# Issuing the stores and the v loads from SyncE, and moving the v loads and the second v cast of one batch, in a fused attention and feed-forward kernel

## The chip, the cores and the metric

The kernel runs on one core of one Trainium2 chip. The metric is the device time of one execution in microseconds (us). Each kernel was run several times, in rounds in which it alternates with the kernel before on the same chip. The span that a profile shows is about 1.8 us shorter than the device time of the same run.

Engines have short names in the profile: PE is TensorE (matmuls), PEld its weight loads, DVE is VectorE, ACT is ScalarE, POOL is GpSimd, SP is SyncE. A trailing q (ACTq, SPq) means the instruction queue of that engine, here the issuing of a DMA. L427 is line 427 of the kernel file. From its first edit on, the changed file is one line shorter, so L427 of before is L426 of after, and so on; from the last edit on, near the end of the file, it is three lines longer. The experiments have line numbers of their own.

## The reference, cut to what matters

```python
# per batch b (8) and head (8): cosine-weighted linear attention over 576 positions, head size 64
q_p = [relu(q) * cos, relu(q) * sin];  k_p = the same of k
kv  = k_p^T @ v;  z = sum over positions of k_p
attn = (q_p @ kv) / (q_p @ z + 1e-6)
# then on all 4608 tokens (512 channels, 1536 hidden)
xn  = attn / rms(attn) * g
out = (silu(xn @ w_gate) * (xn @ w_val)) @ w_out
```

Inputs and output are float32; the kernel multiplies in bfloat16.

## The kernel before: the parts that matter

The work is cut into blocks. Block b is the feed-forward network of the 512 main tokens of batch b; block 8 is that of the last 64 tokens of every batch. A block has 16 slots: slots 0 to 11 compute one slice of the hidden layer each (four matmuls into psG, four into psV, a silu on ScalarE giving sg, a product on VectorE giving hT), and slots 12 to 15 compute one quarter of the output each (12 matmuls into psC, a copy to osb on ScalarE, a store). The attention of batch b+1 is woven into the slots of block b, and the loads for batch b+2 too.

```python
def load_piece(which, b, p):
    if which != "q":
        eng = nc.scalar if (which, b) == ("v", 3) else nc.sync
        load_kv(which, b, p, p + 1, eng=eng)
    ...

def v_cast(eng, b, r0=0, r1=4, j0=0, j1=NJ):      # raw v (float32) -> vvm (bfloat16)
    ...
def kvz_mm(b, banks, rs=(0, 4)):                  # kv and z: psA <- vvm, kpm (72 matmuls)
    ...
def nd_pe(b, j, pst):                             # numerator, denominator: psA <- kvzs, qpT (8 matmuls)
    ...
def nd_post(b, j, pst):                           # VectorE: rec, reciprocal, xt = numerator * rec
    ...
def x_norm(b, j):                                 # VectorE: xn
    ...
def x_tr_dma(b, j):                               # transpose by DMA, from SyncE: xnT <- xn
    nc.sync.dma_start_transpose(out=x_dst(b, j), in_=xn_of[(b, j)][:, :])

def out_store(eng, blk, j, bank):
    osb = four.tile([P, DM], FP32, name="osb", tag="osb")
    copy(eng, osb[:, :], bank)
    if blk < 8:
        rows = out[blk * S : blk * S + 512, :].rearrange("(p j) m -> p j m", j=4)
        (nc.scalar if blk else nc.sync).dma_start(out=rows[:, j, :], in_=osb[:, :])
    ...

for nb in range(2, B):                            # attention of batch nb, in block b
    b = nb - 1
    ...
    if nb == 3:
        vb, vn = b, 1
    ...
    at(vb, vn, "post", v_cast, V, nb, *LOW)
    at(vb, vn + 1 + (nb == 3), "post", v_cast, V, nb, *HIGH)
    ...
for nb in range(3, B):                            # loads of batch nb, in block b
    b = nb - 2
    for i, which in enumerate(("k", "v", "q")):
        for p in range(5 if which == "q" else 4):
            n = (p, 7 + p, 6 + p)[i] if b == 1 else 5 * i + p
            at(b + n // 16, n % 16, "post", load_piece, which, nb, p)
```

Batch 3 is the exception in this schedule. Its v is loaded in four pieces by ScalarE in slots 7 to 10 of block 1, and its second cast (HIGH) follows the first by two slots, where in the other batches it follows by one.

## Time and profile before

| | before |
|---|---|
| device time | 330.03 us median of 3 runs, 330.01 to 330.08 |
| span of the profile | 328.8 us (the profiled run took 330.61 us, 0.6 us more than the median) |
| TensorE, VectorE, ScalarE busy | 97%, 56%, 54% |
| TensorE idle between 60 and 314 us | 1.63 us and 1.23 us |

The page gives the busy times of the engines (microseconds, share of the span, number of instructions) and the shares of the chain of work that ended last.

```profile
PE 319.3 (97%) x2445; PEld 162.3 (49%) x2445; DVE 185.7 (56%) x412; ACT 177.8 (54%) x366; POOL 32.2 (10%) x67
PE 86%; DVE 5%; DMA 3%; ACT 3%; issue 1%; ACTq 1%; SPq 0%; DVEq 0%
```

TensorE is nearly always busy, so only the moments in which it waits can pay. Busy time by stretches finds them. The columns are the stretch, its length, and the busy time of each engine; the last three are the granted clock, the DMA share and GB/s.

```profile
80.00:84.00 4.00, 2.37 (x19) 1.12 (x18) 2.92 (x6) 1.39 (x4) 0.55 (x1) 1.00 1.05 257
93.00:117.00 24.00, 22.77 (x199) 11.38 (x198) 16.55 (x34) 12.94 (x26) 2.15 (x4) 1.00 0.80 177
```

The view of waits names the releasers (total us, times, longest us):

```profile
ACT sg L436 <- DMA rq<-in_q_dram: 1.9, 1, 1.9
PE psA L311 <- DVE xt L365: 1.6, 1, 1.6
PE psA L283 <- DVE vvm L266: 1.2, 1, 1.2
```

The timeline shows how they hang together. Columns: start, duration, engine, line, operation, count, and in brackets the idle time before it and its releaser. First gap A, in block 1, slot 12:

```profile
79.10 0.33 ACTq L79 DMA_DIRECT2D rv<-in_v_dram  x1
79.47 1.46 PE L447 MATMUL psC<-wo,hT 128*128 128x512 bf16 x6
79.48 0.60 ACT L436 ACTIVATE sg<-psG 128x512 f32<-128x512 f32 x1 [1.91 <-DMA rq<-in_q_dram]
80.11 0.69 DVE L442 TENSOR_TENSOR hT<-psV,sg 128x512 bf16<-128x512 f32 x1 [2.78 <-ACT sg L436]
80.72 0.74 DVE L388 SCALAR_TENSOR_TENSOR xn<-xt,rs,gb 128x512 bf16<-128x512 f32 x1
81.81 0.69 DVE L365 TENSOR_TENSOR xt<-psA,rec 128x512 f32<-128x512 f32 x1
82.56 0.40 PE L311 MATMUL psA<-kvzs,qpT 128*128 128x65 bf16 x8 [1.63 <-DVE xt L365]
92.34 1.03 PE L427 MATMUL psG<-xnT,wg 128*128 128x512 bf16 x4
```

ScalarE runs its instructions in order. The third load of v could not be issued before 79.10, the silu behind it therefore started late, and from there the delay ran over hT, xn and xt to TensorE. Gap B is in block 2, slot 4:

```profile
98.38 1.03 PE L427 MATMUL psV<-xnT,wv 128*128 128x512 bf16 x4
99.34 0.75 PE L283 MATMUL psA<-vvm,kpm 64*128 64x65 bf16 x36
100.52 0.75 DVE L266 CAST vvm<-rv 128x1152 bf16<-128x1152 f32 x1
101.33 0.75 PE L283 MATMUL psA<-vvm,kpm 64*128 64x65 bf16 x36 [1.23 <-DVE vvm L266]
102.01 1.04 PE L427 MATMUL psG<-xnT,wg 128*128 128x512 bf16 x4
```

The second half of kv of batch 3 needs the HIGH cast, which comes in slot 3 of this block, one slot too late.

### The profile page before, as it was taken

The page shows a single profiled execution, that of the slowest core. Times are in us where ns is not written, and L with a number is a line of the kernel's source. Part 1 is how long each engine was busy: PE and PEld are TensorE (multiplying, and loading weights), DVE is VectorE, ACT ScalarE, POOL GpSimd, SP SyncE. Part 2 cuts the span into 40 slices and gives each one's busy share as a digit, 9 for nine tenths or more (in the row PEclk, how much of TensorE's full clock was granted, in tenths as well). Part 3 has the DMA queues.
Part 4 walks back from the last instruction along what each step waited for, and adds up shares of the span by engine and source line. Part 5 has one row for each costly group of instructions (what it writes and reads, how often), then busy time and mean ns, then how long its engine had stood idle before and what let it go on. Part 6 is the DMA issues. An engine that isn't in the chain of part 4 may idle for free.

```text
span 328.8 us, 6430 instructions
## 1 busy us (share of the span) xinstructions
PE 319.3 (97%) x2445; PEld 162.3 (49%) x2445; DVE 185.7 (56%) x412; ACT 177.8 (54%) x366; POOL 32.2 (10%) x67
## 2 busy tenths in 40 slices
PE   8999999998998999999999999999999999999995
PEld 3587465553444444544454445444554444444443
DVE  5875758776755775577257745773577234203410
ACT  6863875963675447545764576447654233223321
POOL 1660112000100100011001100110011000000000
PEclk9999999999999999999999999999999999999999
DMA  7999999899959676966698588967621400020014
GB/s 262 233 197 266 315 179 335 292 201 262 189 135 208 184 168 189 221 192 165 194 212 197 149 204 198 195 168 206 135 56 32 130 32 0 19 110 1 0 35 96
DMA packets 80338, 53.91 MB, mean 164 GB/s; under 512 B 51377, under 2 KB 67761, under 8 KB 80306
## 3 DMA queue, kind: packets, MB, share of 16 engines
q1 hardware_dynamic: 68176, 39.34, 49.7%
q0 software_dynamic: 6880, 4.72, 10.0%
q10 hardware_dynamic: 5250, 9.44, 9.4%
q8 instruction: 19, 0.31, 0.4%
q14 instruction: 13, 0.11, 0.1%
HBM read 37.75 MB, written 9.44 MB: 144 GB/s over the span
## 4 chain that ended last, share of the span: by engine, by line
PE 86%; DVE 5%; DMA 3%; ACT 3%; issue 1%; ACTq 1%; SPq 0%; DVEq 0%
PE psC L447 26%; PE psG L427 25%; PE psV L427 24%; PE psA L283 3%; PE psA L311 2%; DMA rk<-in_k_dram 2%; PE psG L447 1%; DMA rq<-in_q_dram 1%; PE psG L567 1%; PE psV L567 1%; PE psO L567 1%; DVE vvm L266 1%; DVE qp L212 1%; DVE kpm L212 1%; ACT sg L436 1%
## 5 line engine op out<-in xcount | busy, mean ns | idle before, releaser
L442 DVE TENSOR_TENSOR hT<-psV,sg 128x512 bf16<-128x512 f32 x102 | 70.3, 690 | 95.1 <-PE psV L427 82.0
L436 ACT ACTIVATE sg<-psG 128x512 f32<-128x512 f32 x102 | 60.7, 595 | 65.9 <-PE psG L427 63.9
L427 PE MATMUL psG<-xnT,wg 128*128 128x512 bf16 (+1 forms) x368 | 92.9, 375 | 0.1
L427 PE MATMUL psV<-xnT,wv 128*128 128x512 bf16 (+1 forms) x368 | 92.7, 374 | 0.0
L447 PE MATMUL psC<-wo,hT 128*128 128x512 bf16 x396 | 89.4, 379 | 0.0
L427 PEld LDWEIGHTS <-wv 128*128 128x128 bf16 x416 | 40.7, 98 | 47.4
L447 PEld LDWEIGHTS <-hT 128*128 128x128 bf16 x420 | 40.3, 98 | 46.7
L427 PEld LDWEIGHTS <-wg 128*128 128x128 bf16 x416 | 38.5, 98 | 41.0 <-DVE xnT L266 0.4
L381 POOL TENSOR_TENSOR rs<-ms,mhalf 128x1 f32<-128x1 f32 x36 | 19.8, 551 | 203.0 <-ACT scr L376 203.0
L388 DVE SCALAR_TENSOR_TENSOR xn<-xt,rs,gb 128x512 bf16<-128x512 f32 x36 | 26.8, 746 | 19.1 <-POOL rs L381 19.1
L376 ACT ACTIVATE scr<-xt 128x513 bf16<-128x513 f32 x36 | 22.8, 634 | 25.3 <-DVE xt L365 23.7
L264 ACT COPY osb<-psC 128x512 f32<-128x512 f32 (+1 forms) x33 | 19.0, 577 | 31.9 <-PE psC L447 30.7
L210 ACT ACTIVATE kpm<-rk,tab 128x256 bf16<-128x256 f32 (+1 forms) x78 | 31.9, 476 | 7.0 <-ACT osb L264 5.4
L365 DVE TENSOR_TENSOR xt<-psA,rec 128x512 f32<-128x512 f32 x35 | 24.2, 692 | 1.2
L212 DVE TENSOR_SCALAR kpm<-rk,tab 128x256 bf16<-128x256 f32 (+1 forms) x84 | 22.3, 330 | 2.4 <-DMA rk<-in_k_dram 2.4
L210 ACT ACTIVATE qp<-rq,tab 128x512 bf16<-128x512 f32 x32 | 22.4, 713 | 0.0
L311 PEld LDWEIGHTS <-qpT 128*128 128x128 bf16 x248 | 11.6, 98 | 8.5 <-issue 2.2
L212 DVE TENSOR_SCALAR qp<-rq,tab 128x512 bf16<-128x512 f32 x32 | 15.2, 487 | 0.0
L311 PE MATMUL psA<-kvzs,qpT 128*128 128x65 bf16 x248 | 12.8, 194 | 1.9 <-DVE xt L365 1.6
L427 PE MATMUL psG<-xnt_tail,wg 128*128 128x512 bf16 x48 | 12.3, 379 | 0.0
L427 PE MATMUL psV<-xnt_tail,wv 128*128 128x512 bf16 x48 | 12.3, 379 | 0.0
L283 PEld LDWEIGHTS <-kpm 64*128 64x128 bf16 x576 | 9.9, 95 | 4.7 <-issue 4.1
(89 smaller groups left out, 170.8 us busy)
## 6 DMA issues: line engine op xcount, KB each, us to landing
out_dram<-osb ACTq DMA_DIRECT2D x28, 256.0 KB, 3.1
rk<-in_k_dram SPq DMA_DIRECT2D x20, 288.0 KB, 3.7
rq<-in_q_dram SPq DMA_DIRECT2D x20, 256.0 KB, 4.3
rv<-in_v_dram SPq DMA_DIRECT2D x17, 288.0 KB, 3.1
rk<-in_k_dram SPq DMA_DIRECT2D x2, 1152.0 KB, 8.9
rq<-in_q_dram SPq DMA_DIRECT2D x2, 1024.0 KB, 9.4
rv<-in_v_dram SPq DMA_DIRECT2D x3, 576.0 KB, 9.5
wo<-in_moe_w_out_dram POOLq DMA_DIRECT2D x4, 384.0 KB, 7.9
```

Of the source, the lines that this page charges most:

```text
L210: nc.scalar.activation(out=out_ap, in_=in_ap, func=AF.Relu, scale=scale)
L212: eng.tensor_scalar(out=out_ap, in0=in_ap, scalar1=scale, scalar2=0.0, op0=ALU.mult, op1=ALU.max)
L283: nc.tensor.matmul(banks[c][:, r * E : (r + 1) * E], lhsT=kp_main[b][lo : lo + 64, j, r, :], rhs=vvm[b % 2][lo : lo + 64, r, j, :], start= ...
L311: nc.tensor.matmul(o[:, g, i, :], lhsT=qpT[(b, 0)][:, h, j * P : (j + 1) * P], rhs=kvz_of(b, h), start=True, stop=True,)
L365: nc.vector.tensor_tensor(out=xt[:, 0:DM].rearrange("p (b h d) -> p b h d", b=2, d=D), in0=o[:, :, :, 0:D], in1=rec[:, :, :].unsqueeze(3). ...
L376: nc.scalar.activation(out=scr[:, :], in_=xt[:, 0 : DM + 1], func=AF.Square, scale=1.0 / math.sqrt(DM), accum_out=ms[:, :],)
L381: nc.gpsimd.tensor_tensor(out=rs[:, :], in0=ms[:, :], in1=mhalf[:, :], op=ALU.pow)
L388: nc.vector.scalar_tensor_tensor(out=xn[:, :], in0=x_of[(b, j)][:, 0:DM], scalar=rs_of[(b, j)][:, :], in1=gb[:, :], op0=ALU.mult, op1=ALU. ...
L427: nc.tensor.matmul(pst[bank][:, cols[0] : cols[1]], lhsT=w[:, t, n * P : (n + 1) * P], rhs=x[:, t, cols[0] : cols[1]], start=(t == 0), sto ...
L436: nc.scalar.activation(out=sg[:, :], in_=psG[bank][:, :], func=AF.Silu)
L442: nc.vector.tensor_tensor(out=hTs[blk][:, n, :], in0=psV[bank][:, :], in1=sg[:, :], op=ALU.mult)
L447: nc.tensor.matmul(bank, lhsT=hTs[blk][:, n, j * P : (j + 1) * P], rhs=wo[:, n, :], start=(n == 0), stop=(n == NNT - 1),)
```

## The change

Its intent is to free ScalarE of all DMA issuing in blocks 1 to 8 (but for two stores at the very end, which stay), to load v of batch 3 only after the transposes of batch 2 have been issued, and to have both v casts of batch 3 done before TensorE needs them.

```diff
     def load_piece(which, b, p):
         if which != "q":
-            eng = nc.scalar if (which, b) == ("v", 3) else nc.sync
-            load_kv(which, b, p, p + 1, eng=eng)
+            load_kv(which, b, p, p + 1)
 ...
-            (nc.scalar if blk else nc.sync).dma_start(out=rows[:, j, :], in_=osb[:, :])
+            nc.sync.dma_start(out=rows[:, j, :], in_=osb[:, :])
 ...   # block 8: two stores of 64 rows each
-                nc.scalar.dma_start(
+                nc.sync.dma_start(
 ...
-        at(vb, vn + 1 + (nb == 3), "post", v_cast, V, nb, *HIGH)
+        at(vb, vn + 1, "post", v_cast, V, nb, *HIGH)
 ...
         for i, which in enumerate(("k", "v", "q")):
+            if (which, nb) == ("v", 3):
+                at(b, 13, "post", load_kv, "v", nb, *LOW)
+                at(b, 14, "post", load_kv, "v", nb, *HIGH)
+                continue
             for p in range(5 if which == "q" else 4):
-                n = (p, 7 + p, 6 + p)[i] if b == 1 else 5 * i + p
+                n = (0, None, 6)[i] + p if b == 1 else 5 * i + p
```

More of the change, by code (lines that the diff above doesn't have):

```diff
@@ L69, with load_kv @@
     raw = {}
-    def load_kv(which, b, r0=0, r1=4, j0=0, j1=NJ, eng=nc.sync):
+    def load_kv(which, b, r0=0, r1=4, j0=0, j1=NJ):
         key = (which, b)
@@ L78, in load_kv @@
         src = {"k": k, "v": v}[which]
-        return eng.dma_start(
+        return nc.sync.dma_start(
             out=raw[key][:, r0:r1, j0 * D : j1 * D],
```

## The prediction

> What bounds it now. The page gives TensorE 319.3 us busy of a 328.8 us span (97%) at full granted clock; the chain that ended last is 86% TensorE. Only a gap on TensorE can pay. The table of busy time by stretches shows two between 60 and 314 us: 1.63 us in 80-84 (2.37 of 4.00 busy) and 1.23 us in 93-117 (22.77 of 24.00).
>
> Gap A (80.9 to 82.6 us, block 1 slot 12). The timeline has ScalarE issue the third load of v of batch 3 at 79.10; it stood 1.91 us before its next silu, which the view of waits puts on a DMA of rq. That silu (79.48) delayed hT (80.11), xn (80.72) and xt (ends 82.50), and the eight psA matmuls of tile 3 waited for xt. From the start of psC (79.47) to the next block's first psG (92.34) 12.87 us pass; the chain's clean lengths (10.36 for 48 psC matmuls, 0.24 and 0.37 for the small groups) give 10.97. Gap A costs 1.9 us.
>
> Gap B (100.1 to 101.3, block 2 slot 4). The second half of kvz of batch 3 waited 1.23 us for the HIGH v cast, which VectorE ran in slot 3 (100.52). psV to psG over kvz takes 3.63 us here, 2.23 in block 3: gap B costs 1.4 us.
>
> What changes. (1) No v load in ScalarE's stream in slots 7-10: the silu can start near 77.6. By the traced steps (silu start to hT start 0.63, on to xt end 2.39) xt ends at 80.6; TensorE needs it at 80.8. Gap A closes with 0.1 us to spare. (2) HIGH cast in slot 2: ends near 99.6 in old time; its matmuls are due at 100.0. Gap B closes. (3) 34 stores leave ScalarE, 0.34 to 0.5 us each, some 13 us; ScalarE is 54% busy and no TensorE gap waits on a store: worth nothing. (4) SyncE gains them. In a block of 33.6 us it then issues about 21 us (transposes 1.2 us, loads 0.57 us, stores 0.34 us each). It has room, but issues in order: q pieces of slots 12-13 stand behind stores that wait for osb. In block 2 the last large q piece would issue near 124 instead of 122 us, land near 128.5, and be wanted near 129.3. (5) v of batch 3 in two 576 KB loads would issue near 88 and 89 us and land near 92.5 and 95 (estimate from 4.4 us for such a load of rk and 200 to 250 GB/s); casts come near 95 and 97.
>
> The Trainium skill, "DMA: Bandwidth & Descriptors", section "Issuing engines are not separate DMA queues", says that all issuers share 16 DMA engines and another issuer saves only issue time. The trace shows that issue time, 0.34 us a store; I expect no bandwidth effect.
>
> On the critical path: 1.9 + 1.4 = 3.3 us. Predicted 326.8 us, 326.4 to 328.2 eight times in ten. Chances: faster by over 2% 0.01, within 2% 0.97, slower 0.02.
>
> Right, if: no silu waits for a DMA of rq, psA waits for neither xt nor vvm after 60 us, TensorE stays near 319 us busy in a span near 325.5. Wrong, if: v of batch 3 lands after its cast is due (vvm waits for a DMA near 95 us, hT behind it); q pieces held behind stores make qp wait for rq at the start of blocks 3 to 6; or xt still ends too late.

## The result, and the profile after

| | before | after |
|---|---|---|
| device time, median of 5 runs | 330.01 us (329.73 to 330.08) | 326.83 us (326.63 to 327.37) |
| ratio after/before | | 0.9908 (95%: 0.9893 to 0.9922) |
| span of the profile | 328.8 us | 325.0 us |

A ratio is the mean time of one kernel's fast runs over the mean of the other's fast runs of the same rounds, so it is not quite the ratio of the medians. The gain of 3.18 us (330.01 - 326.83) is 1.0%, and is well clear of the noise.

The same views after. First the page:

```profile
PE 316.5 (97%) x2410; PEld 161.8 (50%) x2445; DVE 185.8 (57%) x412; ACT 176.7 (54%) x366; POOL 31.9 (10%) x67
PE 91%; DMA 2%; ACT 2%; DVE 2%; issue 1%; SPq 1%
```

Only 2410 of the 2445 matmuls have a record here, so the busy time of TensorE is too low. A later profile of the same kernel (e12_change_again) has all 2445 and gives 318.7 us in a span of 325.5 us. The work is the same as before (319.3 us); what went is the waiting. Busy time by stretches says the same, since what is missing here in 93-117 are absent records (216 matmuls; the later profile has 220 in this stretch, and 24.00 us busy):

```profile
80.00:84.00 4.00, 4.00 (x27) 1.98 (x26) 3.03 (x8) 1.54 (x4) 0.55 (x1) 1.00 0.68 160
93.00:117.00 24.00, 23.84 (x216) 11.96 (x218) 17.61 (x38) 12.79 (x27) 2.19 (x4) 1.00 0.93 213
```

These are all the waits of TensorE that the view lists for the whole run, and all of them are in the opening:

```profile
PE psO L466 <- DVE warm L145: 1.2, 1, 1.2
PE psG L566 <- DVE xnT L265: 0.5, 1, 0.5
PE psO L326 <- ACT kvzs L263: 0.4, 1, 0.4
PE psO L254 <- ACT qp L209: 0.3, 1, 0.3
```

The timeline where gap A was, up to the start of block 2:

```profile
77.37 0.58 ACT L435 ACTIVATE sg<-psG 128x512 f32<-128x512 f32 x1
77.98 0.69 DVE L441 TENSOR_TENSOR hT<-psV,sg 128x512 bf16<-128x512 f32 x1 [0.76 <-ACT sg L435]
79.36 1.46 PE L446 MATMUL psC<-wo,hT 128*128 128x512 bf16 x6
79.68 0.69 DVE L364 TENSOR_TENSOR xt<-psA,rec 128x512 f32<-128x512 f32 x1
80.65 0.41 PE L310 MATMUL psA<-kvzs,qpT 128*128 128x65 bf16 x8
85.94 1.19 SPq L406 DMA_TRANSPOSE xnT<-xn  x1
87.79 0.43 SPq L79 DMA_DIRECT2D rv<-in_v_dram  x1
89.45 0.39 SPq L79 DMA_DIRECT2D rv<-in_v_dram  x1
90.44 1.03 PE L426 MATMUL psG<-xnT,wg 128*128 128x512 bf16 x4
```

The silu starts at 77.37 instead of 79.48, xt ends at 80.37, and TensorE reaches its eight matmuls at 80.65 without a wait. From psC to the first psG of block 2 it is now 11.08 us (90.44 - 79.36) instead of 12.87 us, 1.79 us less. Where gap B was:

```profile
96.49 1.03 PE L426 MATMUL psV<-xnT,wv 128*128 128x512 bf16 x4
96.89 0.76 DVE L265 CAST vvm<-rv 128x1152 bf16<-128x1152 f32 x1
97.45 1.33 PE L282 MATMUL psA<-vvm,kpm 64*128 64x65 bf16 x72
98.71 1.04 PE L426 MATMUL psG<-xnT,wg 128*128 128x512 bf16 x3
```

All 72 matmuls run in one piece; psV to psG takes 2.22 us instead of 3.63 us, 1.41 us less. The two together are 3.20 us, against the 3.18 us that were measured.

This agreement is closer than it should be, for the profiled run of before was a slow one, and the spans of the two profiles differ by 3.8 us. Of these, 1.8 us lie at gap A, 1.4 us at gap B, 0.1 us in the opening, and 0.5 us at the very end: from the first psC of block 8 to the end of the span it is 14.7 us before and 14.2 us after. This third part was not looked for. It is 14.5 to 14.7 us in the seven profiles of kernels that load v of batch 3 in four pieces (before, e1, e2, e5, e6, e9, e10), and 14.2 to 14.3 us in the seven that load it in two. Near the end of every trace SyncE checks the completion semaphores of the DMAs one after the other, some 0.06 us each; in before seven checks follow the last landing, in after two. That two loads fewer change the order of these checks is argued from the traces; no run tests it alone.

### The profile page after: what moved, and what is told of

Read it like the earlier page. It is cut to its first block, busy times and chain, and to the rows that moved or that the text cites. A ratio compares the mean times of both kernels' runs of the same rounds, so it can differ in the third digit from the quotient of the medians.

```text
span 325.0 us, 6411 instructions
## 1 busy us (share of the span) xinstructions
PE 316.5 (97%) x2410; PEld 161.8 (50%) x2445; DVE 185.8 (57%) x412; ACT 176.7 (54%) x366; POOL 31.9 (10%) x67
## 4 chain that ended last, share of the span: by engine, by line
PE 91%; DMA 2%; ACT 2%; DVE 2%; issue 1%; SPq 1%
PE psC L446 26%; PE psG L426 26%; PE psV L426 26%; PE psA L282 3%; DMA rv<-in_v_dram 2%; PE psA L310 2%; PE psG L446 2%; PE psG L566 1%; PE psV L566 1%; PE psO L566 1%; ACT kpm L209 1%; PE psV L254 1%; ACT sg L435 0%; SPq L79 0%; PE psA L317 0%
## 5 line engine op out<-in xcount | busy, mean ns | idle before, releaser
L426 PE MATMUL psG<-xnT,wg 128*128 128x512 bf16 (+1 forms) x352 | 90.9, 374 | 0.7
L446 PE MATMUL psC<-wo,hT 128*128 128x512 bf16 x382 | 88.2, 379 | 0.7
```

The source lines that it names most:

```text
L426: nc.tensor.matmul(pst[bank][:, cols[0] : cols[1]], lhsT=w[:, t, n * P : (n + 1) * P], rhs=x[:, t, cols[0] : cols[1]], start=(t == 0), sto ...
L446: nc.tensor.matmul(bank, lhsT=hTs[blk][:, n, j * P : (j + 1) * P], rhs=wo[:, n, :], start=(n == 0), stop=(n == NNT - 1),)
```

## The experiments

The theory is that the gain is two separate gaps of TensorE: A, from a wait in ScalarE's stream, and B, from the place of the HIGH cast. (The half microsecond at the end of the run, above, belongs to neither, and every profile of a kernel with two v loads has most of it.) The stores are worth nothing. The rivals are that the freed time of ScalarE pays, that the gaps have one cause, and, for A, that ScalarE's issuing of loads costs time in itself. Every experiment was run with five rounds. The diffs are against the kernel that each paragraph names.

| run | this, median us | before, median us | ratio (95%) |
|---|---|---|---|
| e1_stores | 330.25 | 330.21 | 1.0005 (0.9976 to 1.0033) |
| e2_cast | 328.78 | 330.21 | 0.9952 (0.9930 to 0.9973) |
| e3_vload | 328.55 | 330.21 | 0.9942 (0.9921 to 0.9964) |
| e4_vload_cast | 327.08 | 330.21 | 0.9900 (0.9881 to 0.9920) |
| e5_act_later | 329.02 | 330.09 | 0.9960 (0.9945 to 0.9974) |
| e6_sp_early | 328.02 | 330.09 | 0.9944 (0.9926 to 0.9962) |
| e7_act_1314 | 326.98 | 330.09 | 0.9902 (0.9889 to 0.9915) |
| e8_v_late | 332.20 | 330.09 | 1.0056 (1.0030 to 1.0082) |
| e9_sp_early_small | 328.05 | 330.04 | 0.9932 (0.9915 to 0.9950) |
| e10_act_later_small | 328.46 | 330.04 | 0.9941 (0.9922 to 0.9960) |
| e11_v_one_later | 327.73 | 330.04 | 0.9934 (0.9898 to 0.9970) |
| e12_change_again | 327.17 | 330.04 | 0.9903 (0.9883 to 0.9923) |

Runs of one group (e1 to e4, e5 to e8, e9 to e12) share one chip and the runs of before.

### e1_stores: the stores alone

```diff
 # against before
-            (nc.scalar if blk else nc.sync).dma_start(out=rows[:, j, :], in_=osb[:, :])
+            nc.sync.dma_start(out=rows[:, j, :], in_=osb[:, :])
 ...   # and the two stores of block 8 likewise
```

> Stores alone on SyncE; v of batch 3 stays on ScalarE, HIGH cast stays in slot 3. Theory (two separate TensorE gaps, neither caused by a store): both gaps stay, about 1.6 us psA<-xt and 1.2 us psA<-vvm in the waits, time 330.0 us within 0.3. Rival (the 13 us of issuing that leave ScalarE are what pays): at least 1 us faster, 329 us or less, and gap A shrinks because ScalarE is freer.

Measured: 330.25 us, ratio 1.0005, and both gaps are there. The rival falls: freeing ScalarE of the issuing of 34 stores is worth nothing that these runs can tell, within 0.3% either way. The profiled run was the slowest of the six (332.53 us; the others lie between 329.81 and 330.83), and its stretches show why. Gap A took 2.18 us in it, and the granted clock of TensorE (third number from the end of the lines by stretches) then stood at half:

```profile
83.03 0.60 PE L311 MATMUL psA<-kvzs,qpT 128*128 128x65 bf16 x8 [2.18 <-DVE xt L365]
83.00:84.00 1.00, 0.97 (x10) 0.69 (x10) 0.57 (x1) 0.72 (x2) 0.11 (x1) 0.50 1.96 327
84.00:85.00 1.00, 1.00 (x4) 0.29 (x2) 0.52 (x1) 0.00 (x0) 0.44 (x1) 0.50 2.70 61
86.00:87.00 1.00, 1.00 (x5) 0.42 (x4) 1.00 (x4) 0.78 (x2) 0.00 (x0) 0.85 0.83 139
```

A gap can cost more than its own length: at half clock for some 3.4 us (82.9 to 86.3), TensorE lost about 1.7 us more, an estimate from these two times. The Trainium skill, "TensorE: Matmul & The Clock Gate", section "Part 1: The HAM clock gate", says that TensorE falls to half clock after at least one idle window of about 3.4 us. Half clock agrees; the length differs, since 2.18 us of waiting sufficed in this run. (The 1.63 us in before left the clock at 1.00.)

### e2_cast: the early HIGH cast alone

```diff
 # against before
-        at(vb, vn + 1 + (nb == 3), "post", v_cast, V, nb, *HIGH)
+        at(vb, vn + 1, "post", v_cast, V, nb, *HIGH)
```

> HIGH cast of batch 3 moved to slot 2 alone. Theory: gap B (psA<-vvm, 1.2 us in the waits, 1.4 us of time) goes and gap A stays: 328.6 us. Rival (the gaps share one cause, the late silu of block 1): B shrinks only with A, time 330.0.

Measured: 328.78 us, 1.43 us less than before. In the waits psA no longer waits for vvm, while psA still waits 1.7 us for xt and the silu 2.0 us for a DMA of rq. Gap B is independent of gap A and is worth what was expected.

### e3_vload: the v loads alone

```diff
 # against before: v of batch 3 in two loads, issued by SyncE, slots 13 and 14; stores and cast unchanged
+            if (which, nb) == ("v", 3):
+                at(b, 13, "post", load_kv, "v", nb, *LOW)
+                at(b, 14, "post", load_kv, "v", nb, *HIGH)
+                continue
```

> v of batch 3 in two loads on SyncE in slots 13 and 14, alone. Theory: gap A (psA<-xt) goes, gap B stays because the HIGH cast is still in slot 3: 330.0 - 1.9 = 328.1 us. Rival (the later landing of v makes the cast wait): psA<-vvm grows above 1.4 us and the time stays above 328.6.

Measured: 328.55 us, 1.66 us less. No silu waits for a DMA, psA does not wait for xt, and the wait of psA for vvm is 1.2 us as before. Gap A goes with the loads alone. The 1.66 us also hold the shorter end of the run (14.3 us in this profile, 14.7 us in before), so by the medians gap A is worth at most 1.7 us rather than 1.9 us, and nearer 1.3 us when the end is taken off. Between the profiles it is 1.8 us.

### e4_vload_cast: loads and cast, stores left on ScalarE

```diff
 # against before: the diffs of e2_cast and e3_vload together
```

> Loads and cast as in the change, all stores left on ScalarE. Theory: the stores are worth nothing, so the whole gain is here: 326.8 us within 0.3, no psA wait after 60 us. Rival (the stores carry part of the gain): 327.5 us or more.

Measured: 327.08 us, 3.13 us less; the sum of e2 and e3 is 3.09 us. Its ratio, 0.9900, is that of the whole change (0.9908, and 0.9903 for e12_change_again). The parts add up, and the stores carry none of the gain.

### e5_act_later: ScalarE keeps the v loads, two of them later

In the built program, nearly every DMA issue of SyncE and ScalarE waits for the completion of an earlier DMA whose completion semaphore it takes over (the first eight do not, nor do some others in the opening and at the end). There are eight such semaphores, shared by both issuing engines in turn. The Trainium skill, "DMA: Bandwidth & Descriptors", section "Why a DMA increments its semaphore by 16 and not by 1", gives a reason for such waits: two DMAs in flight on one semaphore can let a wait pass too early. No run here shows a wait that passed too early; what the traces show is the price of waiting. In before, the third v load took over the semaphore of a q piece that SyncE had issued at 74.57 and that the chain of waits has landing at 79.08, after 4.51 us. At 79.10 the load was issued. This trace thus shows a DMA on one engine's stream holding up another engine's stream.

```diff
 # against before plus the early HIGH cast
-                n = (p, 7 + p, 6 + p)[i] if b == 1 else 5 * i + p
+                n = (p, (7, 8, 11, 12)[p % 4], 6 + p)[i] if b == 1 else 5 * i + p
```

> Before plus the early HIGH cast, with v of batch 3 still four loads on ScalarE, but pieces 3 and 4 in slots 11 and 12 instead of 9 and 10. In the built program every DMA issue waits for the completion of an earlier DMA whose completion semaphore it reuses (eight go round among both issuers); piece 3 waited for a q piece issued near 74.5 and landed at 79.08. Theory (gap A is that wait, not ScalarE's issue time): the four issues still cost ScalarE about 0.38 us each, but silu no longer waits for a DMA of rq and gap A goes: 326.8 us within 0.4. Rival (four issues in ScalarE's stream are what delays it): A stays in part, 327.5 us or more.

Measured: 329.02 us. The theory was half right. Gap A is gone although ScalarE still issues all four loads: its silu starts at 78.40 with no wait for a DMA, and the eight psA matmuls run at 81.68 without a gap. But the time is no better than with the early cast alone (328.78 us), and a new wait has opened at the start of block 2:

```profile
81.56 0.33 ACTq L79 DMA_DIRECT2D rv<-in_v_dram  x1
84.97 0.34 ACTq L79 DMA_DIRECT2D rv<-in_v_dram  x1
92.36 0.82 PE L427 MATMUL psG<-xnT,wg 128*128 128x512 bf16 x3 [0.73 <-DMA xnT<-xn]
```

Block 2 needs the last transpose of batch 2. In before it landed 3.7 us after its issue, in after 2.4 us, here 5.4 us. I call this gap C. In before it did not show, because gap A held back TensorE by more: there the transpose landed at 91.8, and block 2 started at 92.34. It is not the whole loss: from psC to the first psG of block 2 this profile still takes 0.9 us less than before (11.97 against 12.87 us). But it came to that psC 0.9 us later (80.39 against 79.47), and nothing in the edit touches the time before slot 7 of block 1. Why the other runs are slow too stays open.

### e6_sp_early: SyncE issues v in four pieces in slots 7 to 10

```diff
 # against before, with the stores and the cast as in the change
-            eng = nc.scalar if (which, b) == ("v", 3) else nc.sync
+            eng = nc.sync
```

> Change, but v of batch 3 in four loads by SyncE in slots 7 to 10, ahead of the x transposes of batch 2. Theory (only ScalarE's wait mattered; SyncE has room): the x transposes move later by up to 2 us but the last one has about 4 us before block 2 starts, so 326.8 us within 0.4. Rival (v must stand behind the transposes): block 2's first psG waits for xnT, or psA matmuls come late, 327.8 us or more.

Measured: 328.02 us, about 1.0 us above the change (326.98 us for e7_act_1314 on the same chip). This time the rival was right. Gap A is gone, and gap C is there:

```profile
86.26 0.50 SPq L457 DMA_DIRECT2D out_dram<-osb  x1
86.86 1.22 SPq L407 DMA_TRANSPOSE xnT<-xn  x1
92.21 1.04 PE L427 MATMUL psG<-xnT,wg 128*128 128x512 bf16 x4 [1.05 <-DMA xnT<-xn]
```

Of the 1.0 us, 0.4 us lies at the end of the run, which is 14.5 us with four v loads and 14.2 us with two; the rest is what gap C costs. So it is not enough to take the v loads off ScalarE. "Behind the x transposes of batch 2" is a needed part of the change. (The change also makes two loads of the four; no run separates the number of loads from their place.)

### e7_act_1314: the new place, but issued by ScalarE

```diff
 # against after
-                at(b, 13, "post", load_kv, "v", nb, *LOW)
-                at(b, 14, "post", load_kv, "v", nb, *HIGH)
+                at(b, 13, "post", load_kv, "v", nb, 0, 2, 0, NJ, A)
+                at(b, 14, "post", load_kv, "v", nb, 2, 4, 0, NJ, A)
 ...   # A is nc.scalar; load_kv gets back its argument eng
```

> Change, but ScalarE issues the two v loads of batch 3, in slots 13 and 14. Theory (place in the order decides, not the engine): the DMA whose semaphore is reused has landed by then, so ScalarE pays 0.4 us twice and TensorE does not notice: 326.8 us within 0.3. Rival (ScalarE must not issue loads): 327.5 us or more.

Measured: 326.98 us, ratio 0.9902, the same as the change. The place in the order counts, and the issuing engine does not. (Four timed runs, where the others have six.) One margin is thinner: the last transpose took 4.3 us to land here, and 4.1 us in e4_vload_cast, against 2.4 us in the change. Neither cost time. In e7 ScalarE issued a v load 0.95 us before this transpose, in e4 a store 0.26 us after it; what such neighbours do is taken up below.

### e8_v_late and e11_v_one_later: how much room is there behind?

```diff
 # against after, e8_v_late
-                at(b, 13, "post", load_kv, "v", nb, *LOW)
-                at(b, 14, "post", load_kv, "v", nb, *HIGH)
+                at(b, 15, "post", load_kv, "v", nb, *LOW)
+                at(b + 1, 0, "post", load_kv, "v", nb, *HIGH)
 # against after, e11_v_one_later: slots 14 and 15
```

> Change, but the two v loads two slots later (slot 15 of block 1 and slot 0 of block 2). It measures how much room the new place left. In the change they were issued at 87.8 and 89.4 and wanted at 95.2 and 96.9. Here they issue near 92 and 95, land 4 to 6.6 us later, near 97 and 100: the casts wait about 2 and 3 us, hT stands behind them in VectorE's order, and kvz waits: 328 to 331 us. If the landing takes 3 us only, the loss is near 0.5 us.

Measured: 332.20 us, more than was expected. The second load was issued at 95.28 and landed after 6.0 us; the cast waited 3.13 us for it:

```profile
101.33 0.76 DVE L265 CAST vvm<-rv 128x1152 bf16<-128x1152 f32 x1 [3.13 <-DMA rv<-in_v_dram]
102.15 0.76 PE L282 MATMUL psA<-vvm,kpm 64*128 64x65 bf16 x36 [3.63 <-DVE vvm L265]
103.93 1.91 PE L426 MATMUL psV<-xnT,wv 128*128 128x512 bf16 x4
```

The group of four psV matmuls after it takes 1.91 us instead of 1.03 us: the granted clock was 0.50 between 104 and 106 us. After a gap of 3.63 us half clock is as the page on the clock gate says, but it came at about 103.5, 1.3 us after the matmuls had started again. It lasted 3.4 us, so it cost some 1.7 us on top of the wait (an estimate, half of the 3.4 us). Five of the six runs have a mean clock of 0.99 or 0.995 and 331.95 to 333.33 us; the sixth kept a clock of 1.0 and took 329.82 us. That the other four lost their clock in the same place is likely but not shown: a mean does not say where.

> Change, but the two v loads one slot later (14 and 15 of block 1). e8, two slots later, lost 5 us with landings of about 4.5 and 6 us. Here they issue near 89.4 and 91.7 and would land near 94.5 and 97.7; casts are due at 95.2 and 96.9. Expect no wait or one of up to 1 us: 326.8 to 328 us. If it costs over 1 us, the change's place is the last that works.

Measured: 327.73 us, with runs from 326.72 to 331.20. In the profile the HIGH cast waited 0.62 us for its load and psA 0.22 us for the cast. What made the run of 331.20 us slow is not known. (The clock of the profiled run also fell to half for a while in the opening, which has nothing to do with v.) The place that the change chose is nearly the last that works: there the HIGH load lands at about 96.1 (89.45 plus 6.6 us), and its cast starts at 96.89.

### e9_sp_early_small and e10_act_later_small: is it the bytes of v?

Both bring only 2 of 9 columns of each piece of v of batch 3, with the same number of issues, and GpSimd zeroes the rest earlier. Their outputs are wrong, which doesn't matter for the times.

```diff
 # against e6_sp_early (e9) and e5_act_later (e10)
-            load_kv(which, b, p, p + 1, eng=eng)
+            load_kv(which, b, p, p + 1, 0, 2 if (which, b) == ("v", 3) else NJ, eng=eng)
+    for r in range(4):                            # zero columns 2 to 8 in slots 5 and 6 of block 1
+        at(1, 5 + r // 2, "post", v_clear, 3, r, r + 1)
```

> As e6_sp_early (four v loads on SyncE in slots 7 to 10), but each piece brings 2 of 9 columns, 64 KB instead of 288 KB; GpSimd zeroes the rest beforehand, so the result is wrong on purpose. Same number of issues in the same places. e6 lost 1.1 us because block 2's first psG waited 1.05 us for the last x transpose, which took 5.3 us to land. Theory (bytes of v ahead of the transpose in the DMA engines): landing falls to 2.4 to 3.5 us, that wait goes, time as the change, 326.9 us within 0.4. Rival (four more issues in SyncE's order are the cause): the wait stays and the time is 327.8 us or more.

Measured: 328.05 us; e6_sp_early had 328.02 us. The ratios are 0.9932 and 0.9944, and their intervals overlap. Gap C shrank in the profile from 1.05 to 0.53 us but stayed, so my theory of the bytes falls as the whole cause.

> As e5_act_later (v of batch 3 issued by ScalarE in slots 7, 8, 11, 12; early HIGH cast), again with 64 KB pieces and a wrong result on purpose. e5 closed gap A but won nothing, for the last x transpose landed after 5.4 us and psG waited for it. Theory (ScalarE's issuing is harmless when nothing waits; bytes are what e5 paid for): 326.9 us within 0.4. Rival (four loads in ScalarE's stream cost time themselves): 328 us or more.

Measured: 328.46 us, where e5_act_later had 329.02 us (ratios 0.9941 and 0.9960). Gap C went from 0.73 to 0.59 us. The expected 326.9 us was missed here too. The silu again waits for no DMA. Of the 1.29 us to e12_change_again (327.17 us), the profiles account for 0.8 us from psC to the first psG of block 2 (11.84 us against 11.08 us in both profiles of the change), which is gap C and its surroundings, and for 0.5 us at the end of the run. That leaves next to nothing for ScalarE's issuing.

What gap C is made of can be set out from the profiles, one run each. In after, the last transpose is issued 0.03 us after its xn ends, lands 2.4 us later, and block 2 starts 2.1 us after that; this 2.1 us is the slack. The last column names the loads and stores that were issued next to the transpose, with the time from its issue.

| run | issue after the end of xn, us | landing after issue, us | both beyond after, less 2.1 us of slack | gap C in the profile, us | neighbours |
|---|---|---|---|---|---|
| after | 0.03 | 2.4 | none | 0 | stores at -1.9 and +1.3, v load at +1.9 |
| e1_stores | 0.03 | 2.4 | none | 0 | stores at -2.0 and +1.3 |
| before | 0.03 | 3.7 | none | 0 | store at +0.26 |
| e4_vload_cast | 0.03 | 4.1 | none | 0 | store at +0.26, v loads at +1.25 and +2.0 |
| e7_act_1314 | 0.03 | 4.3 | none | 0 | v load at -0.95, stores at -2.0 and +1.3 |
| e5_act_later | 0.03 | 5.4 | 0.9 | 0.73 | v load at -2.0, store at +0.26 |
| e6_sp_early | 0.39 | 5.3 | 1.2 | 1.05 | stores at -0.6 and +1.7 |
| e9_sp_early_small | 1.05 | 4.1 | 0.6 | 0.53 | store at -0.6 |
| e10_act_later_small | 0.03 | 5.2 | 0.7 | 0.59 | v load at -2.0, store at +0.25 |

Both things occur: SyncE gets behind when it has four more loads ahead of the transposes (e6, e9), and the transpose lands more slowly. For the slower landing the stores are the first thing to look at. These are the landings of the last transpose in before and in e1_stores, and then in e4_vload_cast and in after; in each pair only the stores differ:

```profile
DMA to landing us min/median/max: 3.7/3.7/3.7
DMA to landing us min/median/max: 2.4/2.4/2.4
DMA to landing us min/median/max: 4.1/4.1/4.1
DMA to landing us min/median/max: 2.4/2.4/2.4
```

From ScalarE the store goes out 0.26 us after the transpose; from SyncE, whose order puts it behind the transpose, 1.3 us after. In before and e1 the v loads stay early on ScalarE, and they had all landed before this transpose was issued (at 85.7 in before, where it was issued at 88.05). So the stores alone cost it 1.3 to 1.7 us here, which was slack in all four kernels. In e5 and e10 it takes a further 1 to 2 us, and a v load was issued 2.0 us ahead; e10 brings only 2 of 9 columns of v and is hardly faster, so it is not the bytes alone. In e6 and e9 a store stands 0.6 us ahead. No run takes these neighbours away one by one, so this part of gap C stays open.

### e12_change_again: the yardstick

```diff
 # no difference from after
```

> The change itself, as the yardstick of these rounds: 326.8 us within 0.3, block 2 waits for no transpose.

Measured: 327.17 us, ratio 0.9903. Block 2 waits for no transpose, and all matmul records are there.

No experiment beat the change; e4_vload_cast and e7_act_1314 equal it.

## Why the prediction was right, point by point

The predicted time was 326.8 us, the measured one 326.83 us. The two gaps and what closes them were foreseen (the reason of the wait behind gap A was not). That the numbers agree to 0.03 us is luck: the five runs spread over 0.7 us, the term of gap A was too large, and some 0.5 us at the end of the run, which nobody foresaw, made up for it.

- **Gap A.** Predicted to close with 0.1 us to spare and to be worth 1.9 us. It closed, with 0.28 us to spare (xt ends at 80.37, the matmuls start at 80.65). It measured 1.79 us in the two profiles and 1.66 us in e3_vload, of which 0.4 us lies at the end of the run, so the term was too large by 0.1 to 0.6 us.
- **Gap B.** Predicted 1.4 us, measured 1.41 us in the profiles and 1.43 us in e2_cast. The two are independent and add up, as e4_vload_cast shows.
- **The stores are worth nothing.** Right: e1_stores gives 1.0005. The wait of kpm for osb on ScalarE, 5.4 us before, is gone from the list after, and this changed nothing.
- **SyncE has room.** Right. The last large q piece of batch 4 was issued at 120.46 us (about 123.8 in the time of before, where I had said 124) and landed 3.6 us later, at 124.1; its first use is at 125.9.
- **v of batch 3.** I had said landing near 92.5 and 95 and casts near 95 and 97. The loads were issued at 87.79 and 89.45, landed at 92.8 and 96.05, and were cast at 95.17 and 96.89. The HIGH load was thus nearer to being late than I thought, 0.84 us, and e11_v_one_later shows how near.
- **No effect on bandwidth.** Right for the change as it stands, but too broad as reasoning. I gave the closing of gap A to the fact that no v load stands in ScalarE's stream in slots 7 to 10. That is enough for gap A, but not for the gain: e6_sp_early satisfies it and loses 1.0 us, 0.4 us of it at the end of the run and the rest to gap C. What I had not seen is that the last transpose is the next thing to be waited for. Its landing fell from 3.7 us to 2.4 us with the change, and it is the moved stores that did this, not the moved loads (2.4 us in e1_stores, but 4.2 us in e3_vload and 4.1 us in e4_vload_cast). The stores were worth no time all the same, since block 2 waited for this transpose in none of these kernels; the prediction had not weighed that. The section of the DMA page that I cited says that the issuers share the same 16 DMA engines; e7_act_1314 agrees with it (the issuer does not matter), and e6_sp_early shows that the order in which they are given their work does.
- **The wait behind gap A.** I had put it on a DMA of rq without knowing why a load of v should wait for q. It is the completion semaphore that the load takes over, and e5_act_later, where two of the loads come later and take over other semaphores, is rid of the wait while ScalarE still issues all four loads.

## What to carry to other kernels

A DMA issued from a compute engine costs that engine not only the issue (0.33 us here) but also every wait of the issue, such as that for the completion of an earlier DMA whose semaphore is reused (1.9 us here); look at what stands behind it in that engine's order. When a gap of the busiest engine closes, look for the next wait that it hid: here both early places of the v loads that were tried (e5, e6) traded gap A for a late transpose, and only the place behind the transposes gave the whole gain. Moving 34 issues off an engine that was 54% busy paid nothing by itself here, with TensorE at 97%; what it gave was margin, a transpose that landed 1.3 us sooner. And add up the whole span before believing a sum of gaps: here half a microsecond lay where nobody had looked.

## What the Trainium skill lacked or had wrong

- "TensorE: Matmul & The Clock Gate", Part 1, has the clock fall to half after an idle window of about 3.4 us. In e1_stores it fell to 0.50 after a gap of 2.18 us. In the profile of e8_v_late it fell after a gap of 3.63 us, but only 1.3 us after the matmuls had started again.
- "DMA: Bandwidth & Descriptors", section "Issuing engines are not separate DMA queues", counts only issue time for an issuing engine. In before, issuing one load held ScalarE's next silu for 1.91 us, of which 0.33 us was the issue. The page says elsewhere that a semaphore wait happens on the issuing sequencer, but does not draw this conclusion for an engine that also computes.
- No page gives the time to landing of a transpose by DMA from SBUF to SBUF. For the last transpose of batch 2, one 128x512 bfloat16 tile, it was 2.4 us in the change, and 3.7 to 5.4 us in kernels where a store or a load of v was issued less than 1 us before or after it.
